# A fused attention and StarReLU kernel: the first unit's conversions, sums and stores in another order

## The chip, the cores and the metric

The kernel runs on one core of one Trainium2 chip. The metric is the device time of one execution in microseconds, lower is better. The core has five engines, each with its own instruction stream that runs in order: TensorE (PE in the profile; PEld is its loading of weights), VectorE (DVE), ScalarE (ACT), GpSimd (POOL) and SyncE (SP), which here only issues transfers (DMAs). An instruction that waits holds up all that stands behind it on its engine.

## What is computed

```python
kv  = einsum('bhsd,bhse->bhde', k, v)             # 8 batches, 8 heads, 576 rows, 64 wide
o   = einsum('bhsd,bhde->bhse', q, kv)
x   = o / sqrt(mean(o*o, -1) + 1e-6) * g_norm     # then (b, h, s, d) -> (b*s, h*d): 4608 x 512
h   = x @ w_in                                    # w_in 512 x 2048
g   = s * max(h, 0)**2 + b
out = g @ w_out                                   # w_out 2048 x 512
```

q, k, v and g_norm are 32-bit floats. w_in and w_out are generated as 32-bit floats times a NumPy double and arrive as 64-bit floats; the kernel reads each as a pair of 32-bit words and turns it into one 32-bit float on the chip.

## The kernel before, in words

The 4608 rows are worked in nine **units** of 512 rows (`u`). For each unit, the attention gives `xT`, the normalised rows transposed; a first product (`mm1`) gives g in four **steps** `s` of 512 of the 2048 columns; and a second product (`mm2`) gives the output. Both products are 2 by 2 block products in Strassen's manner: seven block products instead of eight, with sums of blocks of the weights and of the data formed ahead on VectorE. In a step they are called `x1`, `z2`, `x6`, `y7`, `x5`, `x3` and `y4` after the PSUM bank (x, y or z) that they add into and the number of the product. `x1`, `x6`, `x5` and `x3` add into the same bank one after the other, and after `x1`, `x6` and `x5` ScalarE copies the bank's state out (L718; the copies are called r1, r2 and r4). A copy must be over before the next product may add to the bank.

Unit 0 is special, because the weights are still coming in. Its steps 0 and 1 (`mm1_plain`, eight **slots** in `slots0`) are plain products that need no sums. Its steps 2 and 3 are the seven-product form and need `sums_w_in(s)` (two halves of two VectorE operations each: `s12` and `s34`) and `x_sums(0)` (two halves of two as well). The squares of g are taken on VectorE, and the affine `s*g + b` on ScalarE (L644). It is put off: a tile goes on the list `to_scale`, and `scale_g()` issues what is on it.

The weights come in 16 **blocks** of 1 MB: 0 to 7 are w_in (two for each step), 8 to 11 the upper half of w_out (tile `w_up`), 12 to 15 its lower half (`w_dn`). Three raw tiles take turns. Converting a block is four instructions: `hi` and `lo` on ScalarE (L225, L230, in place), then `shift` and `plus` on VectorE (L235, L245). The end of `plus(n)` frees the raw tile, and SP then issues the load of block n + 3. After block 15 the three raw tiles go to the two halves of the second batch's k and v (`load_kv(1, 0)`, `load_kv(1, 1)`) and to a temporary of w_out, `t2`.

`more(n)` takes one slice of w_out's product 5 (one VectorE operation). `store_w2(i)` issues two DMAs of 512 KB on SP that write block product i's weights to DRAM for the later units. `loads(1, 0)` and `loads(1, 1)` issue four q loads each on SP.

`mm2(0)` is a list of 14 slots: `x1(0)`, `x1(1)`, `early_5(0)`, `early_5(1)`, `z2(0)`, `z2(1)`, `x6(0)`, `x6(1)`, `y7(0)`, `y7(1)`, `x3(0)`, `x3(1)`, `y4(0)`, `y4(1)`. `z2` reads all of `w_dn`. After `z2(1)` and `x6(1)` stand `t3` and `t4`, which overwrite the tiles of products 1 and 2 with those of 7 and 4. The loop over these slots at the end of the kernel (n counts them) puts work beside them: the last conversions, stores and loads from the lines that the diff touches, and the next unit's attention from `side_of`: `kv_product(1)` after slot 6, transposes of q after slots 7 and 9, and so on. A transpose of q and a product of it share two PSUM banks, so the second pair of transposes waits until VectorE has read the first pair's product (`back`, L557).

The order of the work is the program's order: `tc.manual_schedule()` makes each engine take its instructions as the code issues them. Semaphores are put in by the framework where tiles are shared.

## Time and profile before

| | us |
|---|---|
| time, median of 3 runs (lowest to highest) | 922.75 (922.36 to 923.43) |
| time of the profiled execution | 926.07 |
| its span, first to last instruction | 924.3 |
| TensorE, share of the span busy | 98% |
| VectorE, share of the span busy | 72% |
| ScalarE, share of the span busy | 39% |
| mean granted TensorE clock | 0.992 |

The unit 0 that the change touches lies in the first 145 us of the span. Slots 2 to 7 of the first product run on TensorE from 32 to 53 us, its steps 2 and 3 from 53 to 84 us, the second product from 84 to 151 us. In the timeline a line gives the start, the time, the engine, the line of the code, the operation with its output and inputs, and in brackets how long the engine had been idle and what ended that. In the windows view a line gives a stretch, then the busy time of PE, PEld, DVE, ACT and POOL with the number of instructions, the granted clock of TensorE (1.00 is full speed), the busy share of the DMA engines and GB/s. In the waits view a line gives who waited for whom, the total, the number of times and the longest.

### The profile page before, as it was taken

How to read it: one execution, taken by the hardware profiler on the slowest of the kernel's cores; microseconds unless marked ns; L12 is line 12 of the kernel's file. 1: busy time of each engine (PE TensorE's matmuls, PEld its weight loads, DVE VectorE, ACT ScalarE, POOL GpSimd, SP SyncE). 2: the span in 40 equal slices, each digit the busy share in tenths (PEclk: the TensorE clock that was granted, in tenths of full speed). 3: DMA queues.
4: the chain of work that ended last, by engine and by line, in shares of the span. 5: the costliest groups of instructions: out<-in, count | busy, mean ns of one | idle time of the engine just before them, and what ended most of it. 6: DMA issues, size and time to landing. Idle time of an engine off the chain costs nothing.

```text
span 924.3 us, 19231 instructions
## 1 busy us (share of the span) xinstructions
PE 902.1 (98%) x7506; PEld 827.8 (90%) x7506; DVE 667.4 (72%) x1234; ACT 360.0 (39%) x606; POOL 227.5 (25%) x432
## 2 busy tenths in 40 slices
PE   7988989999999999999999999999999999999998
PEld 6867778888888999899989998999999989999998
DVE  2895747468747895788587857787688868883686
ACT  2866323552135502660168015800572056204610
POOL 2000003502554042650346033703340210021000
PEclk9999999999999999999999999999999999999999
DMA  9663795616982697259734874398438812792275
GB/s 261 219 216 136 210 301 162 195 35 234 391 263 59 189 301 261 63 150 304 254 114 113 303 260 135 85 288 300 133 87 265 298 53 58 249 298 70 57 250 184
DMA packets 120138, 180.34 MB, mean 195 GB/s; under 512 B 29168, under 2 KB 46320, under 8 KB 120048
## 3 DMA queue, kind: packets, MB, share of 16 engines
q1 hardware_dynamic: 101552, 153.00, 53.1%
q0 software_dynamic: 15040, 23.88, 8.7%
q10 hardware_dynamic: 3456, 2.23, 1.0%
q8 instruction: 60, 0.98, 0.4%
q14 instruction: 30, 0.25, 0.1%
HBM read 153.36 MB, written 25.69 MB: 194 GB/s over the span
## 4 chain that ended last, share of the span: by engine, by line
PE 86%; DVE 6%; ACT 3%; DMA 3%; issue 1%; SPq 1%; DVEq 0%; ACTq 0%
PE x_ps L91 45%; PE y_ps L91 24%; PE z_ps L91 9%; PE sx_ps L91 4%; PE y_ps L545 2%; DMA kv_sb<-in_v_dram 2%; ACT w_raw L225 1%; ACT w_raw L230 1%; DMA w_raw<-in_moe_w_in_dram 1%; DVE a L253 1%; PE z_ps L366 1%; PE kv_ps L366 1%; DMA q_sb<-in_q_dram 1%; DVE xs L253 1%; SPq L145 0%
## 5 line engine op out<-in xcount | busy, mean ns | idle before, releaser
L1623 POOL DMA_DIRECT2D q_sb<-in_q_dram x256 | 143.7, 569 | 134.9 <-ACT a L652 62.8
L1210 POOL DMA_DIRECT2D out_dram<-o x110 | 54.8, 505 | 413.9 <-issue 152.7
L91 PE MATMUL x_ps<-w_sb,sub 128*128 128x128 f32 x1176 | 148.8, 276 | 0.6 <-DVE r L250 0.6
L91 PEld LDWEIGHTS x_ps<-w_sb,sub 128*128 128x128 f32 x1176 | 139.8, 192 | 0.9 <-DVE r L250 0.9
L91 PE MATMUL x_ps<-xs,ws 128*128 128x256 f32 x544 | 132.4, 387 | 6.3 <-ACT r L718 6.2
L644 ACT ACTIVATE a<-a,b_col,s_col 128x512 f32<-128x512 f32 x144 | 116.3, 813 | 34.1 <-DVE a L647 27.9
L91 PE MATMUL y_ps<-xs,wb 128*128 128x256 f32 x544 | 128.5, 381 | 0.0
L91 PEld LDWEIGHTS x_ps<-xs,ws 128*128 128x128 f32 x544 | 101.8, 194 | 20.3 <-ACT r L718 7.9
L91 PEld LDWEIGHTS y_ps<-xs,wb 128*128 128x128 f32 x544 | 101.1, 191 | 13.1 <-issue 0.6
L819 ACT COPY a<-x_ps 128x512 f32<-128x512 f32 x28 | 16.4, 584 | 216.2 <-PE x_ps L91 216.0
L91 PE MATMUL x_ps<-xT,wa 128*128 128x256 f32 x336 | 78.4, 382 | 0.1
L250 DVE TENSOR_TENSOR r<-sx_ps,a 128x256 f32<-128x256 f32 x63 | 26.6, 422 | 62.6 <-PE sx_ps L91 62.4
L91 PEld LDWEIGHTS x_ps<-xT,wa 128*128 128x128 f32 x336 | 62.3, 190 | 9.6 <-issue 1.3
L91 PE MATMUL x_ps<-w_sb,a 128*128 128x128 f32 (+1 forms) x432 | 64.9, 299 | 0.0
L91 PE MATMUL y_ps<-w_sb,a 128*128 128x128 f32 (+1 forms) x416 | 62.2, 295 | 0.0
L91 PEld LDWEIGHTS x_ps<-w_sb,a 128*128 128x128 f32 x432 | 59.0, 192 | 3.2 <-issue 0.4
L250 DVE TENSOR_TENSOR a<-y_ps,r 128x512 f32<-128x512 f32 x40 | 27.5, 688 | 45.8 <-PE y_ps L91 33.7
L91 PEld LDWEIGHTS y_ps<-w_sb,a 128*128 128x128 f32 x416 | 56.1, 192 | 2.0
L250 DVE TENSOR_TENSOR r<-x_ps,o 128x256 f32<-128x256 f32 (+1 forms) x84 | 29.7, 353 | 29.4 <-PE x_ps L91 28.8
L91 PE MATMUL y_ps<-w_sb,sub 128*128 128x128 f32 x392 | 49.5, 275 | 0.0
L647 DVE SCALAR_TENSOR_TENSOR a<-a 128x512 f32<-128x512 f32 x67 | 46.4, 692 | 2.3
L253 DVE TENSOR_TENSOR a<-a,a 128x512 f32<-128x512 f32 x72 | 46.8, 685 | 0.4
(185 smaller groups left out, 1519.1 us busy)
## 6 DMA issues: line engine op xcount, KB each, us to landing
w_sb<-w SPq DMA_DIRECT2D x385, 256.0 KB, 4.5
w_raw<-in_moe_w_in_dram SPq DMA_DIRECT2D x8, 1024.0 KB, 6.3
w_raw<-in_moe_w_out_dram SPq DMA_DIRECT2D x8, 1024.0 KB, 5.6
w_sb<-w SPq DMA_DIRECT2D x14, 512.0 KB, 8.8
w<-sub POOLq DMA_DIRECT2D x28, 256.0 KB, 6.3
w_sb<-in_k_dram SPq DMA_DIRECT2D x24, 288.0 KB, 5.0
w_sb<-in_v_dram SPq DMA_DIRECT2D x24, 288.0 KB, 5.1
out_dram<-o POOLq DMA_DIRECT2D x92, 64.0 KB, 4.0
```

The lines of the kernel that those rows point to most:

```text
L91: nc.tensor.matmul(o, lhsT=lhsT, rhs=rhs, start=start, stop=stop, skip_group_check=True)
L225: nc.scalar.activation(hi, hi, AF.Prelu, scale=2.0**-112, alpha=-(2.0**32))
L230: nc.scalar.activation(lo, lo, AF.Copy, scale=2.0**-29)
L250: nc.vector.tensor_tensor(out=o, in0=a, in1=b, op=ALU.add)
L253: nc.vector.tensor_tensor(out=o, in0=a, in1=b, op=ALU.subtract)
L366: nc.tensor.matmul(ps[r][(r ^ l) * HB : (r ^ l) * HB + HB, i, :], lhsT=kv[l][0][rows, j, :], rhs=kv[l][1][rows, j, :], start=(j == 0), sto ...
L545: nc.tensor.matmul(ps[l][32 * p : 32 * p + 32, r, lo:hi], lhsT=bd_kv[b % 2][rows, p, at : at + 32], rhs=st["qT"][rows, p, lo:hi], start=Tr ...
L644: nc.scalar.activation(t, t, AF.Identity, scale=s_col, bias=b_col)
L647: nc.vector.scalar_tensor_tensor(t, t, 0.0, t, ALU.max, ALU.mult)
L819: nc.scalar.copy(g_tile("a11", s), st["x", s])
L1210: queues[s % 2].dma_start(out=view[b, jj, :, cols], in_=st[name, j][s * w : s * w + w, cols])
L1623: load()
```

## The change

No instruction is added or taken away. `convert` is split: `raw(i)` is ScalarE's part (hi, lo) and `convert(i)` VectorE's (shift, plus), so that the two can stand at different places. Then the order is another:

- In the first product's slots, the sums for step 2 and the x sums go to slots 4 to 6; VectorE's part of blocks 6 and 7 goes behind them, to slots 6 and 7. `raw(6)` and `raw(7)` stay at slots 4 and 5, and `raw(8)` joins at slot 6.
- In steps 2 and 3, each `raw` stands two or three products ahead of its `convert`; the sums for step 3 (`of_w(3, ...)`) stand before block 8's conversion; `scale_g()` is called at six places instead of after each product; block 12 is converted here too.
- Beside the second product, blocks 13, 14 and 15 are converted one slot earlier; the stores of products 1 and 5 are issued first; the second `load_kv` goes ahead of the q loads; the stores of 3 and 2 go ahead of the subtraction that makes product 6's tile.

```diff
+    def raw(i):
+        hi(i)
+        lo(i)
+
     def convert(i):
-        for step in (hi, lo, shift, plus):
-            step(i)
+        shift(i)
+        plus(i)
 
     def first_unit():
+        sums = {}
+
+        def of_w(s, k):
+            if k == 0:
+                sums[s] = sums_w_in(s)
+            sums[s][k]()
+
+        of_x = x_sums(0)
+        beside = {
+            1: [partial(raw, 3), partial(convert, 3)],
+            2: [partial(raw, 4), partial(convert, 4)],
+            3: [partial(raw, 5), partial(convert, 5)],
+            4: [partial(raw, 6), partial(of_w, 2, 0), of_x[0]],
+            5: [partial(raw, 7), partial(of_w, 2, 1), partial(g_s1, 0)],
+            6: [partial(raw, 8), of_x[1], partial(convert, 6)],
+            7: [partial(convert, 7)],
+        }
         for n, slot in enumerate(slots0):
             if n > 1:
                 out_of = slot()
                 if out_of:
                     out_of()
-            if n == 4:
-                g_s1(0)
-            if n in (1, 2, 3, 4, 5):
-                convert(n + 2)
-            if n == 6:
-                s12, s34 = sums_w_in(2)
-                s12()
-                x_sums(0)[0]()
-            if n == 7:
-                s34()
-                x_sums(0)[1]()
+            for fn in beside.get(n, []):
+                fn()
             scale_g()
         a, b = (mm1(0, s) for s in (2, 3))
-        s12, s34 = sums_w_in(3)
-        for step in (
-            [a["x1"], lambda: g_s1(1), partial(convert, 8)],
-            [a["z2"], partial(more, 8)],
-            [a["x6"], s12],
-            [a["y7"], partial(convert, 9)],
-            [a["x5"], s34],
-            [b["x1"], partial(convert, 10)],
-            [a["x3"]],
-            [b["z2"], partial(more, 9)],
-            [a["y4"], a["y4_square"], partial(convert, 11)],
-            [b["x6"], a["x3_s1"]],
-            [b["y7"], partial(more, 10)],
-            [b["x5"], partial(more, 11)],
+        for fn in (
+            a["x1"], partial(g_s1, 1), partial(of_w, 3, 0),
+            a["z2"],
+            a["x6"], partial(of_w, 3, 1), partial(raw, 9), scale_g,
+            a["y7"], partial(convert, 8),
+            a["x5"], partial(raw, 10),
+            b["x1"], partial(convert, 9), scale_g,
+            a["x3"], partial(more, 8),
+            b["z2"], partial(raw, 11),
+            a["y4"], a["y4_square"], partial(convert, 10),
+            b["x6"], a["x3_s1"], scale_g,
+            b["y7"], partial(convert, 11),
+            b["x5"], partial(raw, 12), partial(more, 9), partial(more, 10), partial(more, 11),
+            partial(convert, 12), scale_g,
         ):
-            for fn in step:
-                fn()
-            scale_g()
+            fn()
         return b
...
             if u == 0:
                 if n == 0:
+                    store_w2(1, 5)
                     for name in ("x3", "y4", "y4_square"):
                         last[name]()
-                    convert(12)
+                    raw(13)
                     scale_g()
-                    last["x3_s1"]()
-                    store_w2(1)
-                elif n == 1:
                     convert(13)
                     load_kv(1, 0, convp, tag="raw", bufs=3)
+                    raw(14)
+                    last["x3_s1"]()
+                elif n == 1:
+                    convert(14)
+                    load_kv(1, 1, convp, tag="raw", bufs=3)
+                    raw(15)
                     loads(1, 0)
                     loads(1, 1)
                 elif n == 2:
-                    convert(14)
-                    load_kv(1, 1, convp, tag="raw", bufs=3)
-                    store_w2(5)
-                elif n == 3:
                     convert(15)
                     t2 = convp.tile([P, 4 * R * D], FP32, name="w_t2", tag="raw", bufs=3)
                     W2_AT[6] = t2[:, : FC // 2 * HN].rearrange("p (f n) -> p f n", n=HN)
                 elif n == 4:
+                    store_w2(3, 2)
                     sub_w_out(6, 3, 5)
-                    store_w2(3, 2, 6)
+                    store_w2(6)
```

## The prediction

> **What bounds the kernel now.** I read the page first, then two stretches of the windows view, then who waited for whom on TensorE, then the timeline around each of its gaps.

> ```profile
> PE 902.1 (98%) x7506; PEld 827.8 (90%) x7506; DVE 667.4 (72%) x1234; ACT 360.0 (39%) x606; POOL 227.5 (25%) x432
> ```
> ```profile
> 0.00:130.00 130.00, 112.26 (x831) 95.86 (x832) 82.20 (x128) 67.62 (x103) 6.68 (x18) 0.95 0.73 220
> 130.00:925.00 795.00, 789.87 (x6676) 731.93 (x6674) 585.18 (x1107) 292.40 (x503) 220.87 (x414) 1.00 0.62 191
> ```

> TensorE is the bound, and after 130 us it is idle for 5 us of 795. What an order of work can win lies before 130 us: 18 us idle, of which 6 lie in the first 33 us, which the change leaves alone. The waits of TensorE between 30 and 145 us:

> ```profile
> PE x_ps L91 <- ACT r L718: 6.2, 3, 2.9
> PE kv_ps L366 <- DMA kv_sb<-in_v_dram: 3.0, 1, 3.0
> PE z_ps L91 <- DVE w_dn L245: 2.2, 1, 2.2
> ```

> So five gaps: 2.86, 0.90 and 2.43 us for a ScalarE copy, 2.16 us for the last conversion, 3.02 us for k and v. The timeline at the first (step 2's x6):

> ```profile
> 57.32 0.69 DVE L691 TENSOR_TENSOR a<-a 128x512 f32<-128x512 f32 x1
> 58.05 0.81 ACT L644 ACTIVATE a<-a,b_col,s_col 128x512 f32<-128x512 f32 x1 [3.17 <-DVE a L691]
> 58.77 0.56 ACT L718 COPY r<-x_ps 128x512 f32<-128x512 f32 x1
> 59.39 3.59 PE L91 MATMUL x_ps<-xs,ws 128*128 128x256 f32 x8 [2.86 <-ACT r L718]
> ```

> The copy's input was there at 54.8; it stands on ScalarE behind an affine that waits for a VectorE square. The same eight matmuls take 1.89 us elsewhere and 3.59 here; the clock says why:

> ```profile
> 59.40:59.60 0.20, 0.20 (x1) 0.20 (x2) 0.20 (x1) 0.20 (x1) 0.00 (x0) 1.00 0.00 0
> 59.80:60.00 0.20, 0.20 (x2) 0.20 (x1) 0.20 (x2) 0.20 (x1) 0.00 (x0) 0.50 0.00 0
> 63.20:63.40 0.20, 0.20 (x3) 0.17 (x2) 0.20 (x1) 0.00 (x0) 0.00 (x0) 1.00 0.00 0
> ```

> The clock column is 0.50 from 59.6 to 63.0, and in the same view from 80.1 to 83.5, 107.4 to 110.8 and 121.1 to 124.4. These starts lie on one grid of 3.41 us, and the 3.41 us ahead of each hold 2.0 to 2.9 us of idle TensorE; the 0.90 us gap brings no such stretch. So each long gap costs its idle time plus 1.7 us. The last two gaps:

> ```profile
> 104.69 1.22 DVE L245 CUSTOM_DVE_ANT_0 w_dn<-w_raw,w_dn 128x2048 uint16<-128x2048 uint16 x1
> 105.97 1.13 PE L91 MATMUL z_ps<-w_dn,a 128*128 128x256 f32 x4 [2.16 <-DVE w_dn L245]
> ```
> ```profile
> 102.55 9.26 SPq L145 DMA_DIRECT2D q_sb<-in_q_dram  x8
> 111.91 0.57 SPq L107 DMA_DIRECT2D kv_sb<-in_k_dram  x1
> 112.52 0.47 SPq L107 DMA_DIRECT2D kv_sb<-in_v_dram  x1
> ```

> Block 15 is converted too late for z2(0), and the second k/v load is issued behind eight q loads that hold the SP queue for 9.3 us; it lands at 119.8.

> [...] I use landing times (4.8 to 7.9 us for w_out's blocks) and not issue times.

> **Durations used**, from start to start: VectorE 512-element operation 0.61 us, 0.72 where the next reads its result; shift 0.83, plus 1.14 to the next operation and 1.23 to its own end; ScalarE copy 0.47, hi 1.05, lo 1.06, affine 0.72; TensorE 1.73 us for eight matmuls, 3.45 for sixteen. Nothing is added: each engine's instructions are the same in number, only their order differs.

> **Slots 4 to 7.** ScalarE runs as before to the relu of slot 6 at 52.74; hi 8 and lo 8 now follow (block 8 was issued at 46.75; landed by 54.7 at worst), which ends before 58. VectorE: slot 4's square at 46.67 stays; s1, s2, xs5, xs6 then start at 47.28, 48.00, 48.61 and 49.33, slot 5's relu and square at 49.94 and 50.66, s34 and g_s1(0) from 51.27 to 53.1. Slot 6's square stays at 53.34, since ScalarE sets it. Then come the two x sums (53.95, 54.56), shift 6 and plus 6 (55.17, 56.00), slot 7's relu and square (57.14, 57.86). Before, that square was at 57.32: between the squares stood four sums (2.65 us) and now two sums and a conversion (3.19). So the sums come sooner, but the first gap does not close: affine 58.59, copy 59.31, x6 at 59.93, 0.54 us later, and the half clock stays to 63.0. y7 starts at 63.2 instead of 62.77: **0.43 us lost**.

> **The rest of steps 2 and 3.** The step-2 copy for x5 now has no conversion's wait ahead of it on VectorE or ScalarE: it ends at 63.9, and x5 starts behind y7 at 64.93 instead of 65.69. From there each group of eight follows the last, if its copies are in time. hi 9, lo 9 run at 63.8 and 64.8 (block 9 is issued when plus 6 ends, 57.2, and has 6.5 us), affine 65.9, copy r4 to 67.3, needed by x3 at 68.39. hi 10, lo 10 from 67.4, step 3's r1 copy at 69.5 to 70.1, needed at 73.57. hi 11 at 72.7 (issued 67.0), lo 11, r2 copy 75.4 to 76.0, needed by step 3's x5 at 77.02. Before, x5 started at 80.48 behind a conversion; the third gap goes and its half clock too. x1(0) of the second product starts at 78.75 instead of 83.79; w_up's last block is done at 79.8, and the matmuls that read it come at 81.3. **5.04 us ahead.**

> **The second product.** VectorE: shift and plus 12 at 82.8 and 83.7, so block 15 is issued at 84.9. ScalarE: hi 13 at 86.1, hi 14 at 88.9, hi 15 at 91.5 or when block 15 lands (90.5 to 92.8), lo 15 one later; plus 15 ends near 95.5. z2(0) starts at 101.06 − 5.04 = 96.0 and needs it at its thirteenth matmul, 98.6. So the fourth gap (2.43 us from z2(1)'s start, 1.7 of clock) goes: x6(0) at 102.9 instead of 112.08, **9.2 ahead**.

> **The SP queue.** In order: block 15 at 84.9, stores of products 1 and 5 (2.1 MB, moved ahead), first k/v load from plus 13 at 89.4, second from plus 14 at 92.2, then the eight q loads, then stores 3, 2, 6. From block 15 to the second k/v load are 1.05 + 2.1 + 2.3 = 5.45 MB. Between 114 and 130 the queue moved about 0.30 MB/us, which gives 18 us and some 2 us to land: 105. kv_product needs it at 107.6. So the fifth gap goes (3.1 us, and 1.7 of clock behind it): the q transposes after x6(1) start at 112.4 instead of 126.33, **13.9 ahead**. The q loads land by 110.

> What is late next is VectorE's t4: it overwrites product 2's tiles, so it waits until their store has landed. 8.6 MB from block 15 on took 94.66 to at most 129.6 before, with 4 us in which the queue stood; without those, from 84.9, about 116. VectorE reaches t4 at 115.5, and the transposes that free PSUM for the next q transposes stand behind it with about 1 us to spare. I take 0.5 us of loss there (bounds: 0, and 3 with its clock). **Sum: 13.9 − 0.5 = 13.4 us.** From the profiled span 924.3 to 910.9, from its run of 926.07 to 912.7. The median shown, 922.75, is 3.3 below that run; the gaps are taken to be in both, so 909.4.

> **Rivals.** (1) The transfers set the pace: DMA keeps the pace that it had from block 15 to the first v load before (3.25 MB in 15.6 us, issued from 94.7, landed at 110.3, which is 208 GB/s). Then the second k/v load lands at 111.1: 3.5 us idle and 1.7 us of clock come back, the 0.5 at t4 falls away; gain 8.7, 914.0. For it: q loads and stores blocked the queue for 4.0 and 5.1 us before; against: DMA then waited for VectorE and idled at 109 to 111. (2) hi waits for its block on ScalarE with the copies behind it. Blocks 9 and 11 cost nothing up to a landing time of about 7.4 us; at the 9.4 us of the first w_in loads x3 waits 1.8 us, 3.5 with the clock: gain 10, 912.8. Against: nothing else is in flight at 57 to 85 but one or two blocks. (3) Slower: the two stores ahead of k and v drain slowly. kv_product waits a microsecond for each that the second load is late, and 1.7 once; the gain is gone when it lands after 119.3, which is under 158 GB/s. At 140 GB/s it lands at 123.8: 16.2 + 1.7 − 13.4 = 4.5 us slower, 927.3. For it: 102 GB/s stood in the slice of the q loads; against: stores alone moved 280 to 297 at 125 to 136. (4) The change does half of what it says: already in the forecast, since its first part wins nothing at the first gap.

> **How the numbers follow.** Forecast 0.62, rival 1 0.20, rival 2 0.07, no change (several of these together) 0.03, rival 3 0.08. The predicted time is the forecast's, 909.4, its own range 908.2 to 911. With rivals 1 and 2 the range is 908.0 to 915.0. Faster by over 0.2% (1.85 us, about what a measurement of this kernel can tell) 0.89, within it 0.03, slower 0.08.

> **What would show it.** Right: a first gap of about 3.4 us at 56.5, one half-clock stretch behind it and no other up to 130; x5 of step 3 near 77, x1(0) near 79, z2(0) unbroken, kv_product unbroken near 107. Wrong: x6 starting well before 59; a gap at x3, x5 or z2(0) behind a ScalarE copy or L245; kv_product waiting for v; TensorE idle at the second pair of q transposes behind VectorE; or new idle time after 130.

## The result and the profile after

The kernel after takes 912.09 us (median of 4 runs, 910.47 to 912.53) beside 922.88 us before (922.36 to 923.43): a ratio of 0.988 with a 95% interval of 0.9863 to 0.9897, or 10.8 us less. In a second comparison, later (e5), it was 911.40 (5 runs) beside 924.40 (11 runs): 0.9858, 0.9837 to 0.9879, 13.0 us less. The profiled execution has a span of 910.6 us, against 924.3 before: 13.7 us less, where 13.4 were forecast. So the profiled executions agree with the forecast to 0.3 us, while the first medians fall 2.6 us short of it: 912.09 lies above the forecast's own range of 908.2 to 911 and inside the wider one of 908.0 to 915.0. The experiments show a part of the reason.

The first page of the kernel after, the engines' busy time:

```profile
PE 896.9 (99%) x7506; PEld 824.6 (91%) x7506; DVE 667.3 (73%) x1234; ACT 359.5 (39%) x606; POOL 227.5 (25%) x432
```

The windows view of the same two stretches as before, and the waits of TensorE between 30 and 145 us:

```profile
0.00:130.00 130.00, 120.80 (x983) 104.21 (x984) 90.98 (x142) 69.98 (x109) 7.77 (x20) 0.99 0.80 241
130.00:925.00 795.00, 776.15 (x6525) 720.37 (x6523) 576.30 (x1094) 289.53 (x498) 219.69 (x412) 1.00 0.60 187
```
```profile
PE x_ps L91 <- ACT r L718: 2.9, 1, 2.9
```

Idle time in the first 130 us falls from 17.7 to 9.2 us, by 8.5, and of the five gaps one is left, the first. TensorE's busy time falls too, from 902.1 to 896.9 us for the same 7506 matmuls, since matmuls at half clock count as busy for longer (the eight of x6 for 3.59 us before, where eight at full clock took 1.89). 8.5 and 5.2 us are the whole 13.7 us of the profiled runs. (The second stretch reaches past the end of the shorter span, so its idle time can't be read from it; of the 5 us that the forecast read there before, 0.7 lie past the end.) The timeline at the gap that is left:

```profile
57.96 0.69 DVE L691 TENSOR_TENSOR a<-a 128x512 f32<-128x512 f32 x1
58.68 0.81 ACT L644 ACTIVATE a<-a,b_col,s_col 128x512 f32<-128x512 f32 x1 [2.37 <-DVE a L691]
59.40 0.57 ACT L718 COPY r<-x_ps 128x512 f32<-128x512 f32 x1
60.02 2.78 PE L91 MATMUL x_ps<-xs,ws 128*128 128x256 f32 x8 [2.93 <-ACT r L718]
```

It is the same chain as before: slot 7's square on VectorE, its affine on ScalarE, behind that the copy, behind that x6. The half clock behind it starts inside these matmuls and lasts into y7, the next ones (windows of 1 us; the clock is the third number from the end):

```profile
60.00:61.00 1.00, 0.98 (x5) 0.88 (x6) 1.00 (x2) 0.00 (x0) 0.00 (x0) 1.00 1.01 418
61.00:62.00 1.00, 1.00 (x4) 0.82 (x3) 0.97 (x3) 0.00 (x0) 0.00 (x0) 0.54 1.05 328
63.00:64.00 1.00, 1.00 (x4) 0.79 (x3) 0.97 (x3) 1.00 (x2) 0.00 (x0) 0.50 1.03 422
65.00:66.00 1.00, 1.00 (x6) 0.87 (x6) 0.96 (x2) 1.00 (x2) 0.00 (x0) 1.00 0.00 0
```

The places of the other gaps, in the timeline of the kernel after:

```profile
93.86 1.23 DVE L245 CUSTOM_DVE_ANT_0 w_dn<-w_raw,w_dn 128x2048 uint16<-128x2048 uint16 x1 [0.35 <-ACT w_raw L230]
96.35 3.62 PE L91 MATMUL z_ps<-w_dn,a 128*128 128x256 f32 x16
...
106.80 2.33 PE L366 MATMUL kv_ps<-kv_sb 64*64 64x64 f32 x144
...
117.10 2.50 DVE L253 TENSOR_TENSOR w_dn<-w_dn,w_t 128x512 f32<-128x512 f32 x4 [1.05 <-DMA w<-w_dn]
```

Block 15's conversion ends before z2(0) begins, where it came 2.16 us too late; all 144 matmuls of kv_product run in one piece; and VectorE waits 1.05 us at t4 for the store of product 2, with nothing on TensorE behind it.

### The profile page after: what moved, and what is told of

The parts are those of the page before. It is cut to its first block, busy times and chain, and to the rows that moved or that the text cites. A ratio compares the mean times of both kernels' runs of the same rounds, so it can differ in the third digit from the quotient of the medians.

```text
span 910.6 us, 19226 instructions
## 1 busy us (share of the span) xinstructions
PE 896.9 (99%) x7506; PEld 824.6 (91%) x7506; DVE 667.3 (73%) x1234; ACT 359.5 (39%) x606; POOL 227.5 (25%) x432
## 4 chain that ended last, share of the span: by engine, by line
PE 90%; DVE 5%; DMA 2%; ACT 1%; issue 1%; ACTq 0%; DVEq 0%
PE x_ps L91 47%; PE y_ps L91 26%; PE z_ps L91 9%; PE sx_ps L91 4%; PE y_ps L545 2%; DMA kv_sb<-in_v_dram 1%; PE kv_ps L366 1%; PE z_ps L366 1%; DMA w_raw<-in_moe_w_in_dram 1%; DVE xs L253 1%; DVE xn L578 0%; DVE a L253 0%; PE y_ps L366 0%; DVE sub L253 0%; DVE wa L245 0%
## 5 line engine op out<-in xcount | busy, mean ns | idle before, releaser
L1210 POOL DMA_DIRECT2D out_dram<-o x110 | 54.8, 505 | 401.3 <-issue 152.3
L91 PE MATMUL x_ps<-w_sb,sub 128*128 128x128 f32 x1176 | 148.8, 275 | 0.6 <-DVE r L250 0.6
L91 PEld LDWEIGHTS x_ps<-w_sb,sub 128*128 128x128 f32 x1176 | 139.7, 192 | 0.9 <-DVE r L250 0.9
L91 PE MATMUL x_ps<-xs,ws 128*128 128x256 f32 x544 | 129.9, 382 | 3.0 <-ACT r L718 2.9
L91 PE MATMUL y_ps<-xs,wb 128*128 128x256 f32 x544 | 129.3, 383 | 0.0
L644 ACT ACTIVATE a<-a,b_col,s_col 128x512 f32<-128x512 f32 x144 | 116.1, 812 | 25.5 <-DVE a L647 20.8
L91 PEld LDWEIGHTS x_ps<-xs,ws 128*128 128x128 f32 x544 | 100.2, 191 | 15.8 <-ACT r L718 3.8
L91 PEld LDWEIGHTS y_ps<-xs,wb 128*128 128x128 f32 x544 | 101.5, 192 | 13.5 <-issue 0.6
L91 PE MATMUL x_ps<-xT,wa 128*128 128x256 f32 x336 | 78.4, 381 | 0.1
L91 PEld LDWEIGHTS x_ps<-xT,wa 128*128 128x128 f32 x336 | 62.2, 190 | 9.7 <-issue 1.3
L91 PE MATMUL x_ps<-w_sb,a 128*128 128x128 f32 (+1 forms) x432 | 64.9, 298 | 0.0
L91 PE MATMUL y_ps<-w_sb,a 128*128 128x128 f32 (+1 forms) x416 | 62.2, 295 | 0.0
L91 PEld LDWEIGHTS x_ps<-w_sb,a 128*128 128x128 f32 x432 | 58.9, 192 | 3.3 <-issue 0.4
L91 PEld LDWEIGHTS y_ps<-w_sb,a 128*128 128x128 f32 x416 | 56.1, 192 | 2.1
L91 PE MATMUL y_ps<-w_sb,sub 128*128 128x128 f32 x392 | 49.5, 275 | 0.0
```

The lines of the kernel that those rows point to most:

```text
L91: nc.tensor.matmul(o, lhsT=lhsT, rhs=rhs, start=start, stop=stop, skip_group_check=True)
L644: nc.scalar.activation(t, t, AF.Identity, scale=s_col, bias=b_col)
L1210: queues[s % 2].dma_start(out=view[b, jj, :, cols], in_=st[name, j][s * w : s * w + w, cols])
```

## The experiments

Each kernel was run beside the kernel before on one chip: e1 to e4 on one, e5 to e8 on another, e10 to e12 on the first again. A difference between kernels of different groups goes over the kernel before. The medians, in us:

| kernel | runs | median | before beside it | ratio to before, 95% interval |
|---|---|---|---|---|
| e1 before, again | 21 | 923.09 | 924.23 | 0.9983 to 1.0000 |
| e2 second k/v load behind q | 6 | 917.92 | 924.23 | 0.9911 to 0.9951 |
| e3 second k/v load early, alone | 13 | 923.89 | 924.23 | 0.9983 to 1.0006 |
| e4 slots 4 to 7 as before | 4 | 911.73 | 924.23 | 0.9850 to 0.9888 |
| e5 after, again | 5 | 911.40 | 924.40 | 0.9837 to 0.9879 |
| e6 first product's order alone | 6 | 914.51 | 924.40 | 0.9876 to 0.9918 |
| e7 copy ahead | 5 | 910.00 | 924.40 | 0.9820 to 0.9866 |
| e8 copy and store ahead | 4 | 909.91 | 924.40 | 0.9823 to 0.9870 |
| e10 copies first | 5 | 908.70 | 924.08 | 0.9816 to 0.9846 |
| e11 copies and store first | 4 | 908.24 | 924.08 | 0.9813 to 0.9844 |
| e12 second product's order alone | 5 | 918.23 | 924.08 | 0.9922 to 0.9949 |

### The clock's part: the kernels before and after, many runs

No edit. What was expected of the kernel before:

> The kernel before, unaltered, run again and again. The profiled run of before took 926.07 us and the median 922.75, 3.3 us less; the forecast of 13.4 us was made against the profiled one, the measured gain is 10.8. Theory (phase): the number of half-clock stretches is not a property of the kernel, since the 3.41 us grid lies differently in each run; so some of the four stretches that the profiled run had are missing in other runs. Then the runs differ in steps of about 1.7 us, and the higher the granted clock of a run the shorter its span, by 1.7 us for each 0.0018 of clock (3.41 us at half clock of 924). Rival (profile): the profiled run is longer because it was profiled, and spans of the other runs differ by under 1 us with equal clocks.

Each run has a span and a mean granted clock. Over the 75 runs of the kernel before for which both are known (21 of e1 and 54 beside the other kernels):

| clock | runs | mean span | lowest to highest |
|---|---|---|---|
| 0.992 | 6 | 924.8 | 923.8 to 926.4 |
| 0.994 | 31 | 922.4 | 920.2 to 925.3 |
| 0.995 | 9 | 921.7 | 920.7 to 923.2 |
| 0.996 | 25 | 921.7 | 919.5 to 923.5 |
| 0.998 | 4 | 920.0 | 919.0 to 920.8 |

The profiled run that the forecast was built on had 0.992 and 924.3: its four half-clock stretches are at the slow end of what this kernel does. The profile of e1 (span 919.5, clock 0.996) has the same five gaps, four of them to 0.15 us and one of a different length (1.77 us in kv_product instead of 3.02), and only two half-clock stretches. Its timeline at z2(0) and kv_product:

```profile
105.62 1.13 PE L91 MATMUL z_ps<-w_dn,a 128*128 128x256 f32 x4 [2.15 <-DVE w_dn L245]
106.58 3.62 PE L91 MATMUL y_ps<-w_dn,a 128*128 128x256 f32 x16
...
116.63 1.28 PE L366 MATMUL kv_ps<-kv_sb 64*64 64x64 f32 x72 [1.77 <-DMA kv_sb<-in_v_dram]
```

The same gap of 2.15 us as before (2.16), but the sixteen matmuls behind it take 3.62 us, where they took 5.30. Why is an estimate from the stretches of this run: they begin at 59.6 and 80.05, six times 3.41 us apart. If the grid goes on and a window is one step of it, a window ends at 103.9, and the gap from 103.47 to 105.62 is cut into 0.5 and 1.7 us. The gap of 1.77 us lies whole in one window (114.2 to 117.6) and brings no stretch either. In the profiled run of before, by the same estimate, the window's edges fell so that 1.98 us of that gap were in one window, and the half clock came. So the rival (the run is slow because it was profiled) falls: two profiled executions of this one kernel differ by 4.8 us, one with four stretches and one with two, and over many runs the mean span falls as the clock rises. But the steps are not clean ones of 1.7 us, as was expected; within one clock value spans differ by up to 5 us. One reason is that the gaps themselves differ between runs, as the 1.77 and 3.02 us show; another comes with e3 below.

> The kernel after, unaltered, many runs beside many of before. Theory (phase): one gap of 2.9 us is left, so most runs have one half-clock stretch (clock 0.998) and a few none (1.0, span 1.7 us shorter); before has two to four (0.992 to 0.996 for the most part). The gain lies between 10.8 and 13.4: 12.0, 1.4 below the forecast, since the clock's part of it is smaller than the four stretches of the one profiled run. Rival: the gain is 10.8 again or less, and the runs do not differ by clock.

The kernel after: six runs at 0.998 with a mean span of 910.2, three at 1.0 with 908.7. One stretch or none: 1.5 us, close to the 1.7 of the forecast. The gain of this comparison was 13.0, within what was expected.

### The second load of k and v, put back and alone

The kernel after with the load behind the q loads, and the kernel before with the q loads behind the load:

```diff
 e2, on the kernel after
-                    load_kv(1, 1, convp, tag="raw", bufs=3)
                     raw(15)
                     loads(1, 0)
                     loads(1, 1)
+                    load_kv(1, 1, convp, tag="raw", bufs=3)
 e3, on the kernel before
                     load_kv(1, 0, convp, tag="raw", bufs=3)
-                    loads(1, 0)
-                    loads(1, 1)
 ...
                     load_kv(1, 1, convp, tag="raw", bufs=3)
+                    loads(1, 0)
+                    loads(1, 1)
                     store_w2(5)
```

> The kernel after, with the second load of k and v put back behind the eight q loads on SP. Theory: in before, v landed 17.2 us after the first q load was issued; here that is at about 95.6, so v lands near 112.8, and the second half of kv_product, at 107.9 in after, waits 5 us; with the clock 5.0 to 6.7 us slower than after. Rival (the fifth gap is not worth its time, since the transfers that follow set the pace anyway): within 1 us of after.

It is 6.3 us faster than before, where the whole change (e5) was 13.0, so about 6.7 us of the gain are lost by this one line, the upper end of what was expected (6.2 us beside e4, which ran with it and takes the time of the kernel after). In its profile (waits of TensorE, 30 to 145 us; this run was the fastest of the six):

```profile
PE x_ps L91 <- ACT r L718: 2.9, 1, 2.9
PE kv_ps L366 <- DMA kv_sb<-in_v_dram: 2.6, 1, 2.6
```

The gap in kv_product is back, with a half-clock stretch behind it: 2.6 and 1.7 us. This run, at clock 0.997, shows 4.3 us and not 6; the other five had clocks of 0.994 to 0.996, so more stretches, and no trace shows their gaps. In the kernel after, the place of this load matters.

> The kernel before with one part of the change alone: the q loads go behind the second load of k and v. Theory: the gap of 3.0 us in kv_product closes, and with it up to 1.7 us of half clock: 3.0 to 4.7 us faster than before, if nothing behind it is late. The stores of 5, 3 and 2 still come behind the q loads, so the tile of product 2 may be overwritten later than TensorE needs it: then VectorE waits at t4 and 1 to 3 us are given back at the second pair of q transposes. Rival: no gain, because the q loads are now what kv_product's followers wait for.

In the kernel before it doesn't: 923.89 beside 924.23, no difference that can be told, where 3.0 to 4.7 us were expected. The timeline of e3 shows where the gain went:

```profile
59.58 1.99 PE L91 MATMUL x_ps<-xs,ws 128*128 128x256 f32 x8 [2.71 <-ACT r L718]
...
65.88 1.99 PE L91 MATMUL x_ps<-xs,ws 128*128 128x256 f32 x8 [2.58 <-ACT r L718]
...
114.32 2.33 PE L366 MATMUL kv_ps<-kv_sb 64*64 64x64 f32 x144
...
128.24 2.50 DVE L253 TENSOR_TENSOR w_dn<-w_dn,w_t 128x512 f32<-128x512 f32 x4 [4.67 <-DMA w<-w_dn]
...
131.75 1.25 PE L534 MATMUL qT_ps<-ident,q_sb 128*128 128x128 f32 x8 [2.28 <-DVE q_sb L557]
...
132.84 5.30 PE L91 MATMUL x_ps<-w_dn,a 128*128 128x256 f32 x16
```

kv_product runs in one piece, as expected. But the stores behind the q loads are no earlier than before, VectorE waits 4.67 us for product 2's at t4, and TensorE waits 2.28 us for VectorE at the second pair of q transposes, with half clock behind it. One gap of 3.02 us closed, and the next wait in the same queue opened one of 2.28.

The first two lines show something else, ahead of the edit: the second gap is 2.58 us here, and was 0.90 before:

```profile
65.69 1.99 PE L91 MATMUL x_ps<-xs,ws 128*128 128x256 f32 x8 [0.90 <-ACT r L718]
```

In e3 the first gap brought no half clock: its x6 takes 1.99 us, where it took 3.59. Yet x5 comes 6.30 us after x6 in both, and in e1 and e12, which have the half clock, too. In this order of work x5 waits for its copy, and the copy is not sooner when TensorE is faster. So in the kernel before, the half clock behind the first gap costs nothing: without it the second gap is 1.7 us longer. In the new order x5 follows x6 by 5.25 us with half clock (after) and 3.56 without (e2), and there it costs its 1.7 us.

### The two halves of the change, each alone

e6 is the new `first_unit` with the order beside the second product as before (block 12 converted already); e12 is the reverse.

```diff
 e6, on the kernel after (beside the second product)
                 if n == 0:
                     for name in ("x3", "y4", "y4_square"):
                         last[name]()
                     scale_g()
                     last["x3_s1"]()
                     store_w2(1)
                 elif n == 1:
                     raw(13); convert(13)
                     load_kv(1, 0, convp, tag="raw", bufs=3)
                     loads(1, 0); loads(1, 1)
                 elif n == 2:
                     raw(14); convert(14)
                     load_kv(1, 1, convp, tag="raw", bufs=3)
                     store_w2(5)
                 elif n == 3:
                     raw(15); convert(15)
```

> The new order of the first product alone; beside the second product everything stands as in before, but that block 12 is converted already. Theory: gaps 2 and 3 close, about 5.0 us by the forecast's own step (x1(0) at 78.75 instead of 83.79), and gaps 4 and 5 stay, since conversion 15 still stands behind early_5(1)'s copy and the second k/v load behind the q loads: 3.5 to 5.5 us faster than before. Rival (the first product's order is nearly all of the gain): 9 us or more.

It was 9.9 us faster than before, twice the 3.5 to 5.5 expected and the size that its rival named. Gap 4 is there (2.13 us), as expected, but gap 5 is not, though the load stands behind the q loads. The SP queue and TensorE in e6:

```profile
94.10 0.37 SPq L107 DMA_DIRECT2D kv_sb<-in_k_dram  x1
94.52 0.47 SPq L107 DMA_DIRECT2D kv_sb<-in_v_dram  x1
95.03 7.53 SPq L145 DMA_DIRECT2D q_sb<-in_q_dram  x8
101.95 1.24 PE L91 MATMUL z_ps<-w_dn,a 128*128 128x256 f32 x4 [2.13 <-DVE w_dn L245]
102.67 0.57 SPq L107 DMA_DIRECT2D kv_sb<-in_k_dram  x1
...
111.60 2.33 PE L366 MATMUL kv_ps<-kv_sb 64*64 64x64 f32 x144
```

Before, the first k and v took 2.66 and 1.69 us to issue and the q loads 9.26, here 0.37, 0.47 and 7.53: the second load is issued 8.6 us after the first one instead of 13.8. The difference ahead of them is block 15 and the store of product 1: before, they were issued at 94.7 and 95.1, three microseconds ahead of k and v; here at about 86, since block 12 was converted earlier. The reading that fits is that transfers still under way held up the SP queue, and that their being gone closes gap 5 in e6; no run changed that amount alone. Gap 4 helps: v landed at 109.6, 3.1 us before its matmuls, and without gap 4 and the half clock behind it these would have come 3.8 us sooner. So by this estimate gap 5 would have opened again, by 0.7 us, had gap 4 been closed as well, which is in line with e2.

> The kernel before with the new order beside the second product alone: the first product's slots and steps as in before, block 12 converted beside slot 0 as there. Theory: gap 4 closes, since conversion 15 ends before z2(0) needs it, and gap 5 closes, since the stores of 1 and 5 and both k/v loads are issued ahead of the q loads: 2.2 + 3.0 us and up to 3.4 us of clock, 5 to 8 us faster than before. Together with e6_first_unit_alone (9.9) this is more than the whole change's 13.0, since either part alone closes gap 5. Rival (the parts add up): 13.0 - 9.9, about 3 us.

5.9 us faster than before, so 9.9 + 5.9 = 15.8 is more than the 13.0 of both: the parts overlap, and the traces show where: in gap 5, which either closes. In e12's timeline z2(0) and kv_product run in one piece, and a small new gap stands in early_5(0), which waits for the sum that now comes behind conversion 13:

```profile
97.70 4.58 PE L91 MATMUL y_ps<-w_up,s 128*128 128x256 f32 x20 [0.54 <-DVE s L250]
102.12 3.62 PE L91 MATMUL z_ps<-w_dn,a 128*128 128x256 f32 x16
...
112.57 2.33 PE L366 MATMUL kv_ps<-kv_sb 64*64 64x64 f32 x144
```

### The sums for step 2, put back

```diff
 e4, on the kernel after
-            4: [partial(raw, 6), partial(of_w, 2, 0), of_x[0]],
-            5: [partial(raw, 7), partial(of_w, 2, 1), partial(g_s1, 0)],
-            6: [partial(raw, 8), of_x[1], partial(convert, 6)],
-            7: [partial(convert, 7)],
+            4: [partial(g_s1, 0), partial(raw, 6), partial(convert, 6)],
+            5: [partial(raw, 7), partial(convert, 7)],
+            6: [partial(raw, 8), partial(of_w, 2, 0), of_x[0]],
+            7: [partial(of_w, 2, 1), of_x[1]],
```

> The kernel after with slots 4 to 7 in the order of before: blocks 6 and 7 converted in slots 4 and 5, the sums for step 2 and the x sums in slots 6 and 7; all else as after. Theory: what ends the first gap is slot 7's square on VectorE, behind four sums instead of two sums and a conversion, so x6 starts 0.3 to 0.6 us sooner than in after, and the whole is 0 to 0.6 us faster than after. Rival (the earlier sums are what the change lives on): 2 us or more slower than after.

911.73, with all four runs within those of the kernel after (910.47 to 912.53). The sums' place in slots 4 to 7 is worth nothing that can be told. The gap in its timeline:

```profile
59.00 2.48 PE L91 MATMUL x_ps<-xs,ws 128*128 128x256 f32 x8 [2.78 <-ACT r L718]
```

### Closing the gap that is left

The copy need not stand behind the affine. e7 puts it ahead, and e8 also the store of product 2 ahead of half the q loads:

```diff
 e7, on the kernel after (first product)
             for fn in beside.get(n, []):
                 fn()
-            scale_g()
+            if n < 7:
+                scale_g()
 ...
-            a["x1"], partial(g_s1, 1), partial(of_w, 3, 0),
+            a["x1"], scale_g, partial(g_s1, 1), partial(of_w, 3, 0),
             a["z2"],
-            a["x6"], partial(of_w, 3, 1), partial(raw, 9), scale_g,
+            a["x6"], partial(of_w, 3, 1),
             a["y7"], partial(convert, 8),
-            a["x5"], partial(raw, 10),
+            a["x5"], partial(raw, 9), scale_g, partial(raw, 10),
 ...
-            b["z2"], partial(raw, 11),
+            b["z2"],
             a["y4"], a["y4_square"], partial(convert, 10),
-            b["x6"], a["x3_s1"], scale_g,
+            b["x6"], partial(raw, 11), a["x3_s1"], scale_g,
 e8, also (beside the second product)
                     loads(1, 0)
-                    loads(1, 1)
 ...
+                    store_w2(2)
+                    loads(1, 1)
                 elif n == 4:
-                    store_w2(3, 2)
+                    store_w2(3)
```

> The kernel after with step 2's r1 copy ahead of the affine of slot 7's tile on ScalarE, conversion 9's ScalarE part behind step 2's x5 and conversion 11's behind step 3's x6. Theory: the first gap (2.9 us and its clock) closes, x6 starts near 57.2, and TensorE runs some 3 us earlier up to kv_product. But the store of product 2 still lands near 116, so VectorE waits at t4 for 3 to 4 us and TensorE waits for it at the second pair of q transposes, 2 to 3 us: 0 to 2.5 us faster than after. Rival (only the gap counts): 3 to 4.5 us faster than after.

> As e7_copy_ahead, and on SP the store of product 2 ahead of the second four q loads and of the store of product 3. Theory: the store of product 2 lands some 5 us sooner, VectorE does not wait at t4, and the gain of the closed first gap stays: 2.5 to 4.5 us faster than after. Rival: TensorE then waits in kv_product for v or at a copy in step 3, and it is no faster than e7_copy_ahead.

e7 came out 1.4 us below e5 (their runs overlap), in the range expected, but not for the reason given. e8, of which 2.5 to 4.5 us were expected, is no faster than e7, as its rival said. Nothing on TensorE waits at the q transposes in either. The timeline of e7 shows the gap at another place, step 3's x6:

```profile
67.42 0.81 ACT L644 ACTIVATE a<-a,b_col,s_col 128x512 f32<-128x512 f32 x1 [1.65 <-DVE a L647]
68.14 1.15 ACT L225 ACTIVATE w_raw<-w_raw 128x1024 f32<-128x1024 f32 x1
...
70.20 0.56 ACT L718 COPY r<-x_ps 128x512 f32<-128x512 f32 x1
...
70.81 2.46 PE L91 MATMUL x_ps<-xs,ws 128*128 128x256 f32 x8 [2.11 <-ACT r L718]
```

The edit itself had put an affine that waits for VectorE, and a conversion, ahead of the next copy: the fault of the first gap, one step on. e10 and e11 are e7 and e8 with that one call left out:

```diff
 e10 on e7, e11 on e8
-            a["x5"], partial(raw, 9), scale_g, partial(raw, 10),
+            a["x5"], partial(raw, 9), partial(raw, 10),
```

> As e7_copy_ahead, but the affines of step 2's a11 and a22 tiles stand behind step 3's r1 copy on ScalarE, where e7_copy_ahead had them, with a wait for a VectorE square, ahead of conversion 10 and that copy. Theory: in e7_copy_ahead and e8_copy_and_store_ahead the first gap had only moved to step 3's x6 (2.1 us behind the r1 copy); now the copy ends near 67.7 and x6 of step 3 starts near 68.4 instead of 70.8. Then no gap over 1 us is left up to x1(0), which starts near 74.5 instead of 79.1 in after: 3.5 to 5 us faster than after, unless the store of product 2 (t4) or v is then late, which costs 1 to 3 us of it. Rival (VectorE's own chain of sums, conversions and squares sets the pace from 46 to 84 us, whatever ScalarE's order is): the gap moves once more, and it is within 1 us of e7_copy_ahead.

> As e10_copies_first, with the SP order of e8_copy_and_store_ahead: the store of product 2 ahead of the second four q loads. Theory: if VectorE's wait for that store at t4 reaches TensorE in e10_copies_first, this takes it away, and the kernel is 1 to 3 us faster than e10_copies_first; if it does not reach it, both take the same time to 0.5 us.

908.70 and 908.24: every run of both (908.00 to 908.84) lies below every run of the kernel after (910.47 to 912.53), though the comparison with it goes over the kernel before. The gain over e5 is 2.7 and 3.2 us, under the 3.5 to 5 expected. In e10's profile the copy for step 3 ends at 68.7 and x6 follows without a gap, but the first gap was still 1.84 us there, since ScalarE stood 1.42 us waiting for block 8 ahead of that copy:

```profile
54.50 1.18 ACT L225 ACTIVATE w_raw<-w_raw 128x1024 f32<-128x1024 f32 x1 [1.42 <-DMA w_raw<-in_moe_w_out_dram]
```

In e11's profile none over 0.6 us is left between 30 and 145 us. In e10 VectorE waits 2.1 us at t4 and TensorE not; e11's order on SP takes that wait away, and its 0.5 us can't be told from nothing.

## Why the prediction was right, and where it was off

- **The bound and the gaps.** Right: the gain is the gaps before 130 us and their half clock, 8.5 and 5.2 us. "So each long gap costs its idle time plus 1.7 us" is wrong for the first gap of the kernel before, by e3; the sum is spared that error, since it was worked out from one start to the next. The kernels with gaps put back (e2, e6, e12) lost a part of the gain.
- **Slots 4 to 7 win nothing at the first gap.** Right, by e4. The size was off: a gap of 3.4 us was forecast and 2.93 measured. The copy came when forecast (59.40, 59.31 forecast), but this run lies 0.56 us later than the run before it from ahead of slot 2 on (TensorE at 32.65, 32.09 before), where the change does nothing. Against the slots the copy moved by 0.07 us and not 0.54.
- **Steps 2 and 3.** Right: x5 at 65.27 (64.93 forecast), x1(0) at 79.08 (78.75).
- **The second product.** Right: z2(0) at 96.35 (96.0) in one piece, x6(0) at 103.25 (102.9).
- **The SP queue.** Right in its times: the second v landed at 105.6 (105 forecast), 96.13 plus the 9.5 us to landing that the DMA view gives (its issue took 0.47), and the q transposes came at 112.62 (112.4). The 2 us to land were an estimate; in the trace of before the 24 KB loads of q on SP took 2.0 us from issue to landing. But the step gave a single cause for gap 5, the eight q loads ahead of the second k/v load, and that is not the only one. Moving them closes the gap (e3, though the gain is lost at t4) and putting them back opens it (e2); e6 left them in place and the gap closed too. What fits all of these is how much is still under way on the SP queue when k and v are issued; no run shows it alone.
- **t4.** The 0.5 us taken off was too much: VectorE waited 1.05 us, TensorE not.
- **The profiled pair.** That 13.7 comes so near to 13.4 is in part luck: the later start of the run after took 0.56 us away, and the path behind it was 0.34 us quicker and t4 0.5 us cheaper than forecast.
- **The sum against the median.** This is the term that was mis-sized. "The gaps are taken to be in both" runs holds for the idle time in the main, not for the clock: the forecast takes off three half-clock stretches of 1.7 us, 5.1 us, from a run with four, at clock 0.992, which 6 of 75 runs of the kernel before have. The mean clocks of all runs with a known span are 0.9948 before (75 runs) and 0.9987 after (9 runs). As an estimate from these, with 3.41 us for a stretch, that is 2.8 stretches before and 0.7 after: two go and not three, some 1.5 us less. The mean spans of the same runs, 922.16 and 909.71, differ by 12.4 us. Why the medians of the two comparisons are 10.8 and 13.0 stays open; the four runs of the kernel before in the first (922.36 to 923.43) are faster than its medians beside the experiments (924.08 to 924.40). The 3.3 us by which the profiled run lay above the median could have warned of this.
- **Rivals.** Rival 1 (the transfers set the pace) did not come: DMA moved the 5.45 MB in the forecast's time (block 15 was issued at 85.1, and the second v landed at 105.6). A wait of its kind came in e3, where the store of product 2 was late (4.67 us at t4). Rival 2 did not come in the kernel after: blocks 9 to 14 landed in 4.8 to 5.1 us, block 15 in 5.9. It shows in the profiled run of e10, where block 8 took 8.1. Rival 3 did not come.

## What to carry to other kernels

ScalarE took its instructions in order and so passed a wait on: an affine that waited for VectorE ahead of a copy that TensorE needed cost 2.9 us, and moving one copy only moved the gap until the later copy, too, stood ahead of such work. Parts of one reordering overlap (9.9 and 5.9 alone, 13.0 together), and one part alone may give nothing because the next wait in its queue takes its place, so the next waiter is to be worked out before a gap is counted as won. A stretch at half clock cost nothing where TensorE would have waited for another engine right behind it (in the kernel before x5 came 6.30 us after x6 with it and, in e3, without it). And a profiled run is one draw: set its own time beside the median before its clock losses are summed.

## What the runs showed of the hardware that was not expected

```profile
58.40:58.60 0.20, 0.00 (x0) 0.00 (x0) 0.20 (x1) 0.20 (x1) 0.00 (x0) 0.65 0.53 61
61.60:62.00 0.40, 0.40 (x3) 0.31 (x2) 0.40 (x1) 0.00 (x0) 0.00 (x0) 0.50 0.29 31
65.20:65.40 0.20, 0.20 (x2) 0.14 (x2) 0.17 (x2) 0.20 (x1) 0.00 (x0) 0.78 0.39 82
```

The gap of 2.93 us in the kernel after cost 1.7 us more by its half clock (x5 came 5.25 us after x6, and 3.56 in e2, without it), so a gap like it can be worth closing for its clock too. The half clock is also a part of the spread between runs: the kernel before ranged over 7.4 us in span (919.0 to 926.4, 75 runs), e10, at clocks of 0.999 to 1.0, over 0.7 us (906.3 to 907.0, 5 runs).

Issuing a transfer on SP did not take a fixed time: the same k load took 0.37 us with little under way (e6) and 2.66 us behind 2 MB issued 3 us ahead of it (before), and one store there 5.09 us.
